# A memory-attention and mixture-of-experts kernel on one core: first batch's keys and values in token pieces, w1 in column halves, side steps placed anew

## The chip, the core and the metric

The kernel runs on one core of one Trainium2 chip. The metric is device time in microseconds of one execution, the median over runs; lower is better. All times below are microseconds unless marked ns. Engines are named as the profile names them: PE is the matmul engine (PEld its weight loads), DVE the vector engine, ACT the scalar engine, POOL the GpSimd, SP the engine whose queue issues nearly all DMAs (SPq).

## What is computed

Eight batches of eight heads, 576 tokens, head size 64, with 32 memory slots; then a mixture of eight experts (512 to 1024 to 512) over the 512 values of each token.

```python
a = softmax(phi, axis=tokens)                      # B H S M
k_m, v_m = a^T k, a^T v                            # B H M D
attn = softmax(q k_m^T / 8, axis=M)                # B H S M
x = (attn v_m) as B, S, H*D
# per batch, token after token:
e = argmax(x w_gate) if s == 0 or sigmoid(x w_local) < 0.5 else previous e
out[b, s] = softmax(x w_gate)[e] * (relu(x w1[e]) @ w2[e])
```

With the data used, all tokens of a batch follow the expert of its first token, so each batch loads one expert's w1 and w2, and the loop at the end over further pairs of batch and expert has no turns.

## The kernel before

The output of a batch is x w1 with x = attn v_m, so v_m is multiplied into w1 first (`w_pg`, `w_G`: G = v_m w1) and the hidden layer is attn G. Values are split into a high and a low part (Gh and Gl, ah and al, w2h and w2l), and three products replace one.

For each batch there is a main part on PE, in `moe`: `hidden` (two halves of the tokens, 256 and 320; for each chunk of 128 hidden units six matmuls, then a relu on ACT at L704 and its low part on DVE at L706, from PSUM tiles `ph` of a pool with 3 buffers), `second` for two blocks of 128 tokens (24 matmuls of 512 columns each, then a scaled eviction on ACT, L742), and `second_turned` for the other 320 tokens (four groups of 24 matmuls of 320 columns, each then transposed by DVE into oT). Later batches are prepared by side steps in between:

- the front (`f_...`): `f_colmax` (tree of maxima on DVE), `f_pm`, `f_mc`, `f_pm2`, `f_cx` bring the column maximum to all partitions, `f_sub` and `f_exp`, `f_asum` (tree of sums), `f_pkv` (144 matmul records: k_m and v_m), `f_sums`, `f_rinv`, `f_kvn`, `f_pT`, `f_kvT`, `f_pgg`, `f_ggt`;
- the attention of a batch in two parts of nine blocks of 32 tokens: `k_qT` (DVE transposes), `k_psc` (scores on PE), the softmax steps `k_turn`, `k_mx`, `k_sub`, `k_exp` (ACT), `k_sum`, `k_inv`, `k_mul`, `k_at`, all but one on DVE, then `k_ah` (ACT) and `k_al` (POOL);
- the choice of the expert: `c_pl` (PE), `c_choice` (DVE), `expert` (SP reads the number), then `load1` and `load2` for w1 and w2 in two halves each;
- the weights: `w_pg` (PE), `w_G` (Gh on ACT, L675; Gl on DVE, L676), `w_split` (w2h on ACT, L653; w2l on POOL, L654);
- the gate: `g_pl`, `g_lt`, `g_L`, `g_fresh`, `g_exp`, `g_kept`, `g_carry`, `g_prob`, `g_cols`, `g_present`, mostly short DVE operations.

Their order is written out by hand. `start` issues what comes ahead of the first hidden matmul, with `warm(n)` matmuls on zeros between the steps of PE (L209). All later side steps are put on a list by `at(b, x, f, ...)` in the functions `plan_...`: batch b and a place x in microseconds of the main part's own length (END = 37.8 a batch). While `moe` yields the length of each group of matmuls, the steps whose place is passed are issued. Every engine works off its own queue in that order. Batches 1 to 4 have places of their own in these tables; from batch 5 on they are all alike.

In `start` SP issues phi of batch 0 in two halves of the heads, two small loads of q, k and v by pairs of heads, phi of batch 1, the rest of q and k of batch 1 (into a buffer of the pool `pf`). The gate's weights are loaded by POOL's queue. All loads of SP share one queue. The tiles `raw` for w1 and w2 have three buffers in all.

## Time and profile before

| | |
|---|---|
| median of 3 runs | 463.33 (462.44 to 466.58) |
| the profiled execution | 465.2, its span 463.1 |
| PE busy | 418.2 (90% of the span) |
| DVE busy | 283.8 (61%) |
| ACT, POOL busy | 177.9 (38%), 169.8 (37%) |
| DMA | 82.58 MB, 178 GB/s in the mean |

A row of a timeline has the start, the length, the engine, the line, the operation with its output and inputs, and the count; in brackets is the idle time of the engine ahead of it and what ended it. A row of groups has busy time and the mean ns of one instruction instead. In a table by stretches the columns are the stretch, its length, busy time and count of each engine, the granted clock of PE as a share of full speed, the DMA engines' busy share and their rate. A busy PE is not PE at its peak, since its matmuls overlap; the distance of their starts tells their pace.

### The profile page before, as it was taken

Reading aid. Unit: us, or ns where it says so; the run is one execution under the profiler, and the core shown is the slowest. Engines: PE = TensorE matmul, PEld = TensorE weight load, DVE = VectorE, ACT = ScalarE, POOL = GpSimd, SP = SyncE. Lnnn points to the kernel's source line nnn. Section 1 sums busy time; section 2 is a strip of 40 time slices with the busy share of each in tenths; the row PEclk is TensorE's granted clock in tenths of the full one; section 3 lists DMA queues with packets and bytes.
Section 4 is the critical chain, followed back from the end, with each engine's and each line's share of the span. In section 5 each row is a group of like instructions: output and inputs, shape, how many; then the busy total and the mean of one; then the engine's idle time right before and its main releaser. Section 6 shows DMA issues by size and latency. Waiting matters only on the chain.

```text
span 463.1 us, 10643 instructions
## 1 busy us (share of the span) xinstructions
PE 418.2 (90%) x4188; PEld 340.9 (74%) x4190; DVE 283.8 (61%) x731; ACT 177.9 (38%) x425; POOL 169.8 (37%) x183
## 2 busy tenths in 40 slices
...
GB/s 240 274 313 203 222 163 24 283 143 348 92 134 235 196 268 57 39 282 250 262 154 238 263 233 118 257 215 302 81 279 149 125 104 227 166 24 57 24 36 49
DMA packets 109797, 82.58 MB, mean 178 GB/s; under 512 B 69600, under 2 KB 86000, under 8 KB 109744
## 3 DMA queue, kind: packets, MB, share of 16 engines
...
q14 instruction: 18, 0.15, 0.1%
...
## 4 chain that ended last, share of the span: by engine, by line
PE 44%; DVE 10%; SPq 8%; DMA 4%; issue 2%; ACT 1%; POOL 1%; DVEq 0%; POOLq 0%
PE ph L695 15%; SPq L157 8%; PE po L782 5%; PE po L784 5%; PE po L783 5%; PE po L734 3%; PE po L735 3%; PE po L736 3%; DMA kv_t<-in_k_dram 3%; DVE qT L364 1%; PE psc L391 1%; DMA att_d<-at 1%; PE pg L664 1%; DVE h L706 1%; PE po L756 1%
## 5 line engine op out<-in xcount | busy, mean ns | idle before, releaser
L654 POOL TENSOR_TENSOR w2l<-raw,w2h 128x512 fp32r<-128x512 f32 x64 | 81.7, 1294 | 30.9 <-ACT w2h L653 27.0
L695 PE MATMUL ph<-ah,Gh 128*128 128x256 f32 (+1 forms) x256 | 80.3, 314 | 8.5 <-DVE h L706 8.5
L706 DVE SCALAR_TENSOR_TENSOR h<-ph,h 128x320 fp32r<-128x320 f32 (+2 forms) x104 | 53.3, 522 | 46.1 <-ACT h L704 45.9
L695 PE MATMUL ph<-al,Gh 128*128 128x256 f32 (+1 forms) x256 | 77.0, 301 | 0.0
L695 PE MATMUL ph<-ah,Gl 128*128 128x256 f32 (+1 forms) x256 | 77.0, 301 | 0.0
L782 PE MATMUL po<-h,w2l 128*128 128x320 f32 x224 | 72.7, 324 | 0.0
L784 PE MATMUL po<-h,w2h 128*128 128x320 f32 x224 | 70.3, 314 | 0.0
L783 PE MATMUL po<-h,w2h 128*128 128x320 f32 x224 | 70.3, 314 | 0.0
L704 ACT ACTIVATE h<-ph 128x320 fp32r<-128x320 f32 (+1 forms) x96 | 46.5, 488 | 53.6 <-PE ph L695 50.3
L447 POOL TENSOR_TENSOR al<-at,ah 128x576 fp32r<-128x576 f32 x16 | 23.2, 1451 | 105.9 <-ACT ah L443 105.9
L734 PE MATMUL po<-w2h,h 128*128 128x512 f32 (+1 forms) x152 | 61.6, 405 | 0.0
L695 PEld LDWEIGHTS ph<-ah,Gh 128*128 128x128 f32 x256 | 49.7, 194 | 15.3 <-DVE h L706 10.3
L735 PE MATMUL po<-w2l,h 128*128 128x512 f32 (+1 forms) x152 | 58.8, 387 | 0.0
L736 PE MATMUL po<-w2h,h 128*128 128x512 f32 (+1 forms) x152 | 58.4, 384 | 0.0
L789 POOL TENSOR_TENSOR oT<-oT,gT 128x320 f32<-128x320 f32 x28 | 21.8, 778 | 95.9 <-DVE oT L788 91.8
L695 PEld LDWEIGHTS ph<-al,Gh 128*128 128x128 f32 x256 | 49.7, 194 | 0.0
L695 PEld LDWEIGHTS ph<-ah,Gl 128*128 128x128 f32 x256 | 49.5, 193 | 0.0
L782 PEld LDWEIGHTS po<-h,w2l 128*128 128x128 f32 x224 | 43.0, 192 | 6.0 <-issue 5.5
L653 ACT ACTIVATE w2h<-raw 128x512 fp32r<-128x512 f32 x64 | 38.7, 624 | 12.9 <-DMA raw<-in_moe_w_dram 7.3
L783 PEld LDWEIGHTS po<-h,w2h 128*128 128x128 f32 x224 | 43.0, 192 | 0.2
L784 PEld LDWEIGHTS po<-h,w2h 128*128 128x128 f32 x224 | 43.0, 192 | 0.0
L734 PEld LDWEIGHTS po<-w2h,h 128*128 128x128 f32 x152 | 29.3, 193 | 16.0 <-issue 11.3
...
## 6 DMA issues: line engine op xcount, KB each, us to landing
raw<-in_moe_w_dram SPq DMA_DIRECT2D x16, 1024.0 KB, 6.4
...
```

The lines of the kernel that those rows point to most:

```text
L157: nc.sync.dma_start(out=st.qt[p0 : p0 + 32, h], in_=qv[h, g, j])
L653: nc.scalar.activation(h, src, AF.Copy)
L654: nc.gpsimd.tensor_tensor(out=l, in0=src, in1=h, op=ALU.subtract)
L695: nc.tensor.matmul(pv[:, c - c0], lhsT=lt[:, g, cs], rhs=rt[:, g, s0 : s0 + n], start=(i == 0), stop=(i == 5),)
L704: nc.scalar.activation(hc[:, :, 0:n], pv, AF.Relu)
L706: nc.vector.scalar_tensor_tensor(out=hc[:, :, o : o + z - a], in0=pv[:, :, a:z], scalar=0.0, in1=hc[:, :, a:z], op0=ALU.max, op1=ALU.subtract,
L734: nc.tensor.matmul(po[:, c0:c1], lhsT=h[:, c, th], rhs=hi, start=(c == 0), stop=False)
L735: nc.tensor.matmul(po[:, c0:c1], lhsT=h[:, c, th], rhs=lo, start=False, stop=False)
L736: nc.tensor.matmul(po[:, c0:c1], lhsT=h[:, c, tl], rhs=hi, start=False, stop=(c == FC - 1))
L782: nc.tensor.matmul(po[:, 0:n], lhsT=lo, rhs=h[:, c, 0:n], start=(c == 0), stop=False)
L783: nc.tensor.matmul(po[:, 0:n], lhsT=hi, rhs=h[:, c, 0:n], start=False, stop=False)
L784: nc.tensor.matmul(po[:, 0:n], lhsT=hi, rhs=h[:, c, n : 2 * n], start=False, stop=(c == FC - 1))
```

## The change

1. **Keys and values of batch 0** are loaded right after phi, all heads at once, in two pieces of the tokens (`PIECES`: six and three of each group of nine). `f_sub` and `f_exp` become `f_piece`, `f_asum` becomes `f_asum_piece`, and `f_pkv` runs over a piece's tokens. The small loads of q and the rest of it come behind, then phi of batch 1. k of batch 1 goes to the ordinary buffer, so its load waits for `f_pkv` of batch 0.
2. **The gate's weights** are loaded by SP instead of POOL, between the two loads of q.
3. **w1** is loaded in halves of its columns (all four blocks of rows, 512 columns) instead of halves of its rows, so `w_pg(n)` reads half n alone.
4. **The six matmuls of a hidden tile** come in the order Gh ah, Gl ah for both groups, then Gh al twice; they were Gh ah, Gh al, Gl ah for each group. In the first batch `k_al` is done for each group by itself.
5. **The evictions of `second`** in batches 0 to 6 become a step of their own, `t_evict`, with a place.
6. **The places** of all side steps of batches 0 to 4 are rewritten, and `start` has another order, with 14 warm matmuls instead of 52. `w_pg(0)` comes ahead of the first hidden tile and `w_pg(1)` behind it.

The core of the diff, with a line or two of the tables:

```diff
-        nc.gpsimd.dma_start(out=wg[:, :, 0:E], in_=w_gate.rearrange("(h p) e -> p h e", h=HG))
-        nc.gpsimd.dma_start(out=wg[:, :, E : E + 1], in_=w_local.rearrange("(h p) o -> p h o", h=HG))
+
+    def gate_weights():
+        nc.sync.dma_start(out=wg[:, :, 0:E], in_=w_gate.rearrange("(h p) e -> p h e", h=HG))
+        nc.sync.dma_start(out=wg[:, :, E : E + 1], in_=w_local.rearrange("(h p) o -> p h o", h=HG))
...
+    PIECES = (slice(0, 6), slice(6, 9))
...
+    def f_piece(st, i):
+
+        x = st.pt[:, :, PIECES[i]]
+        c = st.cx.unsqueeze(2).to_broadcast([P, HG, PIECES[i].stop - PIECES[i].start, M])
+        nc.vector.tensor_tensor(out=x, in0=x, in1=c, op=ALU.subtract)
+        nc.scalar.activation(x, x, AF.Exp)
...
-        raw = pw.tile([P, 2, F], F32, tag="raw", name="raw1", bufs=3)
-        nc.sync.dma_start(out=raw, in_=w1v[:, 2 * i : 2 * i + 2])
+        raw = pw.tile([P, HG, F // 2], F32, tag="raw", name="raw1", bufs=3)
+        nc.sync.dma_start(out=raw, in_=w1v[:, :, F // 2 * i : F // 2 * (i + 1)])
...
-                    rhs=st.raw1[h // 2][half[g], h % 2, 512 * n : 512 * n + 512],
+                    rhs=st.raw1[n][half[g], h],
...
-                        for lt, rt in ((G[0], ah), (G[0], al), (G[1], ah)):
...
+                    steps = [(x, ah, g) for g in range(NG) for x in G] + [(G[0], al, g) for g in range(NG)]
...
+    def t_evict(st, t):
+        o, p = st.ot[t]
+        p = p.rearrange("p (dc j l) -> p dc j l", j=4, dc=4)
+        nc.scalar.activation(by_chunk(o), p, AF.Copy, scale=st.g[0][:, t : t + 1])
...
-        x, y, p = {1: (25.4, 25.5, 32.5), 2: (12.4, 12.5, 22), 3: (9, 9.9, 17)}.get(n, (3.6, 9.9, 14))
+        x, y, q, p = {1: (22.9, 23, 23.1, 31), 2: (17.1, 17.2, 17.3, 26), 3: (12.1, 18, 12.2, 21)}.get(
+            n, (3.6, 9.9, 10, 14)
+        )
...
         fetch_phi(s, True)
         gate_constants()
+        for i in range(2):
+            fetch_kv(s, piece=PIECES[i])
         q0 = fetch_q0()
         next(q0)
-        for hs in pairs:
-            fetch_kv(s, parts=((0, hs), (1, hs)))
+        gate_weights()
+        next(q0)
         fetch_phi(n, False, pf, "oT")
-        next(q0)
-        fetch_kv(n, pf, "h256", ((0, slice(0, HG)),))
-
-        warm(12)
+
+        warm(10)
```

How it moves instructions, at the three places of which the prediction speaks. The lines of the changed kernel are its own: L692 is `w_pg`, L722 `hidden`, L704 Gl, L732 the relu's low part, L660 and L670 the loads of w1 and w2.

On PE, the end of `start`: psc is the last part of batch 0's scores, wp the warm matmuls, pg `w_pg`, ph `hidden`. Before, twelve warm matmuls and both halves of `w_pg` stand there, and each half reads both tiles of w1:

```order
L391 MATMUL psc<-qT,kvT 32x288 x8
L209 LDWEIGHTS wz
L209 MATMUL wp<-wz 128x512
...
L664 MATMUL pg<-raw_397,kvT 32x512 x4
L664 MATMUL pg<-raw_399,kvT 32x512 x4
...
L695 MATMUL ph<-ah,Gh 128x256
L695 MATMUL ph<-al,Gh 128x256
L695 MATMUL ph<-ah,Gl 128x256
```

Now:

```order
L415 MATMUL psc<-qT,kvT 32x288 x8
L692 MATMUL pg<-raw_389,kvT 32x512 x8
L722 MATMUL ph<-ah,Gh 128x256
L722 MATMUL ph<-ah,Gl 128x256
...
L722 MATMUL ph<-al,Gh 128x256 x2
...
L692 MATMUL pg<-raw_391,kvT 32x512 x8
L722 MATMUL ph<-ah,Gh 128x256
```

The warm matmuls are gone, one half of `w_pg` with one tile of w1 is ahead of the hidden matmuls, and the other stands behind twelve of them.

On DVE, the same place: at is the end of the softmax of the first part, sc and mx the softmax of the last part, Gl belongs to `w_G`, phi_t to `f_sub` of batch 1, h to the relus. Before:

```order
L439 STREAM_TRANSPOSE at<-sc 128x2x256
L404 STREAM_TRANSPOSE sc<-psc 128x288 x2
L414 TENSOR_REDUCE mx<-sc 128x18
L418 TENSOR_TENSOR sc<-sc,mx 128x576
L676 TENSOR_TENSOR Gl<-pg,Gh 128x512 x4
L258 TENSOR_TENSOR phi_t<-phi_t,cx 128x576 x2
L706 SCALAR_TENSOR_TENSOR h_586<-ph,h_586 128x2x256
L427 TENSOR_REDUCE sm<-sc 128x18
```

Now:

```order
L463 STREAM_TRANSPOSE at<-sc 128x2x256
L704 TENSOR_TENSOR Gl<-pg,Gh 128x512 x2
L428 STREAM_TRANSPOSE sc<-psc 128x288 x2
L438 TENSOR_REDUCE mx<-sc 128x18
L442 TENSOR_TENSOR sc<-sc,mx 128x576
L732 SCALAR_TENSOR_TENSOR h_521<-ph,h_521 128x2x256
L451 TENSOR_REDUCE sm<-sc 128x18
L704 TENSOR_TENSOR Gl<-pg,Gh 128x512 x2
L732 SCALAR_TENSOR_TENSOR h_521<-ph,h_521 128x2x256
L263 TENSOR_TENSOR phi_t<-phi_t,cx 128x576
```

The first half of Gl stands right behind at, ahead of three softmax steps of the last part; the second half and one `f_sub` stand among the relus (the other `f_sub` is ahead of this place).

On SP, from the w2 load of batch 1 on: raw_1105 and raw_1351 are its halves before (raw_1029 and raw_1211 now), q_t is q of batch 2, att_d and out_dram are stores, phi_t and kv_t the loads for batch 3. Before:

```order
L642 DMA raw_1105<-in_moe_w_dram 128x2x512
L157 DMA q_t<-in_q_dram 32x18x32 x16
L452 DMA att_d<-at 128x1152
L135 DMA phi_t<-in_phi_dram 128x4x288
L135 DMA kv_t<-in_k_dram 128x4x576
L135 DMA kv_t<-in_v_dram 128x4x576
L642 ISA
L642 DMA raw_1351<-in_moe_w_dram 128x2x512
```

Now:

```order
L670 DMA raw_1029<-in_moe_w_dram 128x2x512
L162 DMA q_t<-in_q_dram 32x18x32 x16
L851 DMA out_dram<-ot 128x512
L480 DMA att_d<-at 128x1152
L670 ISA
L670 DMA raw_1211<-in_moe_w_dram 128x2x512
...
L140 DMA phi_t<-in_phi_dram 128x4x288
L140 DMA kv_t<-in_k_dram 128x4x576
L140 DMA kv_t<-in_v_dram 128x4x576
```

The second half of w2 has passed three large loads.

From batch 5 on the order of all engines is the one of before, with t_evict where the eviction stood.

327 lines of the change are left out of this document (183 added, 144 removed), and 3 rows, old and new, of the table b.

## The prediction

> **What bounds the kernel now.** I read the table by stretches first, cut where a batch's first hidden matmul starts (batch 0 at 38.32, batch 1 at 105.48, batch 2 at 171.86, batch 3 at 233.66, then every 47.6). Columns: length, then busy us of PE, weight loads, DVE, ACT, POOL, then the granted clock, DMA share and rate.
>
> ```profile
> core 0: us, PE busy (x) PEld busy (x) DVE busy (x) ACT busy (x) POOL busy (x), PEclk, DMA share, GB/s
> 0.00:38.32 38.32, 31.63 (x397) 16.20 (x399) 20.05 (x54) 9.91 (x21) 4.76 (x29) 0.96 0.83 269
> 38.32:105.48 67.16, 57.05 (x691) 46.72 (x684) 40.04 (x99) 24.46 (x60) 28.05 (x32) 0.92 0.64 173
> 105.48:171.86 66.38, 54.54 (x543) 43.83 (x542) 42.76 (x120) 25.90 (x72) 23.22 (x22) 0.92 0.72 212
> 171.86:233.66 61.80, 52.07 (x513) 42.81 (x512) 43.26 (x98) 22.59 (x54) 21.85 (x20) 0.94 0.58 173
> 233.66:281.29 47.63, 47.48 (x509) 39.94 (x508) 34.81 (x87) 21.78 (x52) 22.52 (x21) 1.00 0.72 216
> ...
> 376.53:463.10 86.57, 80.56 (x538) 71.53 (x536) 35.62 (x103) 29.74 (x63) 24.30 (x22) 0.98 0.29 92
> ```
>
> Two regimes. From batch 3 on PE has no idle to speak of: 47.63 a batch, full clock, nothing to win by placing. Before that a batch takes 62 to 67 for the same work, and the first hidden matmul comes only at 38.32. Batches 0 to 2 together take 195.3.
>
> What they would take without stalls: three times 47.63 is 142.9, and one more f_pkv, g_pl, f_sums, k_psc and small steps than three of the later batches, since the fronts get ahead here. The groups of the fourth batch's stretch (busy, mean ns of one):
>
> ```profile
> L280 PE MATMUL pkv<-kv_t,phi_t 64*32 64x128 f32 x144 | 2.2, 271 | 0.0
> L391 PE MATMUL psc<-qT,kvT 64*32 64x288 f32 x32 | 2.1, 415 | 0.2 <-DVE qT L364 0.2
> L484 PE MATMUL pl<-at,ggt 128*32 128x160 f32 (+1 forms) x16 | 0.7, 292 | 0.0
> ```
>
> That is 2.2 + 1.0 (16 of the 32 psc) + 0.7, with about 1 for the small steps: 5. The floor is 148, the loss 47. PE's timeline shows where it sits; in brackets is the idle time before a row and who ended it:
>
> ```profile
> 69.32 0.69 PE L391 MATMUL psc<-qT,kvT 64*32 64x288 f32 x8 [2.47 <-DVE gs L602]
> 70.85 1.18 PE L391 MATMUL psc<-qT,kvT 64*32 64x288 f32 x8 [0.84 <-DVE qT L364]
> 96.70 0.63 PE L280 MATMUL pkv<-kv_t,phi_t 64*32 64x128 f32 x21 [2.21 <-issue]
> 142.41 1.15 PE L484 MATMUL pl<-at,ggt 128*32 128x160 f32 x14 [3.71 <-DVE at L439]
> 187.42 0.48 PE L239 MATMUL pm<-ident,cm 128*128 128x128 f32 x1 [3.76 <-DVE cm L222]
> ```
>
> A side step stands in PE's order before its DVE input is ready, and all matmuls behind it wait. Each gap costs twice, because the clock drops after it; rows around the gap at 69.32:
>
> ```profile
> 66.46 0.39 PE L736 MATMUL po<-w2h,h 128*128 128x512 f32 x1
> ...
> 72.98 0.63 PE L736 MATMUL po<-w2h,h 128*128 128x512 f32 x1
> 73.41 0.63 PE L734 MATMUL po<-w2h,h 128*128 128x512 f32 x1
> ...
> 74.53 0.39 PE L734 MATMUL po<-w2h,h 128*128 128x512 f32 x1
> 74.75 0.39 PE L735 MATMUL po<-w2l,h 128*128 128x512 f32 x1
> ```
>
> Starts are 0.43 apart instead of 0.22 until 74.5, some 2.5 us after work came back.
>
> **The change, part by part.**
>
> *Start up to the first hidden matmul.* The chain of before:
>
> ```profile
> 13.37 1.84 PE L280 MATMUL pkv<-kv_t,phi_t 64*32 64x128 f32 x60 [0.26 <-DMA kv_t<-in_v_dram]
> 21.62 0.24 PE L458 MATMUL pl<-ggt,at 128*1 128x8 f32 x4 [0.38 <-DVE at L439]
> 23.84 0.99 SPq L632 DMA_DIRECT2D raw<-in_moe_w_dram  x2
> raw<-in_moe_w_dram SPq DMA_DIRECT2D x1, 1024.0 KB, 5.2
> 31.27 0.68 ACT L443 ACTIVATE ah<-at 128x576 fp32r<-128x576 f32 x1 [1.39 <-DVE at L439]
> 32.04 1.40 POOL L447 TENSOR_TENSOR al<-at,ah 128x576 fp32r<-128x576 f32 x1 [28.10 <-ACT ah L443]
> 34.75 1.90 PE L664 MATMUL pg<-raw,kvT 64*32 64x512 f32 x18
> 37.30 1.09 PE L664 MATMUL pg<-raw,kvT 64*32 64x512 f32 x14 [0.65 <-DVE Gl L676]
> 38.32 0.39 PE L695 MATMUL ph<-ah,Gh 128*128 128x256 f32 x1
> ```
>
> Keys and values now stand right behind phi on SP, ahead of the q ends and the second phi, and f_pkv follows tokens: I take 2 us off the wait at 13.37 (bounds 0, since pieces of 3 tokens are runs of a third of the length, and 3.5). c_pl moves behind a k_q0 on PE, where eight warm matmuls stood: 0 (up to +2 if q lands late; the k_q0 that waits would hold c_pl, the choice and the w1 load). So w1 goes out near 22. Its first column half suffices for w_pg(0) and needs the 5.2 of one load, not both: about 27 instead of 34.75, where twelve warm matmuls also stood. Then it no longer sets the start. What comes late next is DVE: from the choice to the first half of at took until 31.2, through the second phi's maximum and the softmax. It begins 2 sooner and gets one f_sub more, so ah ends near 30 instead of 31.95. Gh waits for it on ACT; from pg at 34.75 to the first hidden matmul now go 3.6 with the second half of pg between, so with one half I give Gh and Gl 2.3 behind ah. al, 1.40 in one piece on POOL, now comes in two pieces and is read last by each hidden tile, so it sets nothing. First hidden matmul at 32.3, **-6.0** (bounds -8.5, if the 2 us are 3.5 and no clock is lost, and -1, if f_pkv gains nothing, q lands late and the clock drops). w_pg(1) then falls behind that point: **+1.1** (row 37.30).
>
> *SP's queue in the start.* Three steps move there. The two gate-weight loads leave POOL and stand ahead of q: two issues, and many short runs for pgg, which runs only behind f_pkv, so there is some 3 us of cover; without it they hold pgg and c_pl. k of batch 1 loses its own buffer and waits for f_pkv of batch 0 (PE), ahead of the expert's value load: queued behind it is the w1 load. f_pkv ends some 7 us before that load is due, so the wait is over by then: 0 (0 to +2 if f_pkv is late). w1 in column halves has runs of half the length, 2 KB; one load of 1024 KB took 5.2 with 4 KB runs, and I leave it there.
>
> *Fewer warm matmuls.* 38 of 52 go. PE will have gaps of 1 to 4 us in the start, and by the rows at 72.98 some of its work there runs at half pace. f_pkv is 144 records, 4.4 us at the 1.84 for 60 above, and one w_pg 1.1; with k_q0 and k_psc I estimate 11 us of matmul work ahead of the first hidden matmul. After one gap the pace was back in 2.5 us, so I count 1 to 2 lost in the -6.0 and the rest in its upper bound. [...]
>
> *Batch 0.* The second softmax, f_sub, w_G, gate steps and relus (L706) share DVE up to the two k_qT, for which k_psc waits.
>
> ```profile
> 38.32:70.80 32.48, 24.63 (x323) 21.14 (x316) 21.00 (x58) 15.82 (x43) 15.60 (x20) 0.95 0.71 187
> ```
>
> DVE is busy 21.0 of 32.5 there. Now it gets k_turn, k_mx, k_sub of the last part, from ahead of 38.32, and f_asum from POOL, and loses one f_sub. By the 0.76 of a 576-column transpose (L364, below) that is 2.4, and 1.4 for the tree's 1024 columns, against 0.8: 24.0. w_split leaves ACT's way until 7.3, k_at and w_G come sooner. PE is busy 24.6 in the stretch and comes to that k_psc six matmuls of 0.22 sooner now: 23. If DVE is never held up the stall is 1, if it idles for 11.5 as now it is 12; I take 6 for the batch.
>
> *Second w2 load, batch 1.* Rows of SP, ACT and PE:
>
> ```profile
> 85.99 16.30 SPq L157 DMA_DIRECT2D q_t<-in_q_dram  x16
> 105.40 1.78 SPq L642 DMA_DIRECT2D raw<-in_moe_w_dram  x2
> 117.26 0.63 ACT L653 ACTIVATE w2h<-raw 128x512 fp32r<-128x512 f32 x1 [7.34 <-DMA raw<-in_moe_w_dram]
> 119.15 0.63 PE L695 MATMUL ph<-ah,Gh 128*128 128x320 f32 x1 [4.45 <-DVE h L706]
> ```
>
> ACT stood 7.3 us on w2, the relus queued behind it, PE lost 4.45 and ran slow. In the new order that load goes ahead of phi, k and v, so this stall goes whole. The new limit in batches 1 and 2 is DVE in the hidden stage:
>
> ```profile
> L706 DVE SCALAR_TENSOR_TENSOR h<-ph,h 128x320 fp32r<-128x320 f32 x56 | 26.9, 486 | 20.6 <-ACT h L704 20.6
> L706 DVE SCALAR_TENSOR_TENSOR h<-ph,h 128x512 fp32r<-128x512 f32 x32 | 21.9, 686 | 23.2 <-ACT h L704 23.0
> L364 DVE STREAM_TRANSPOSE qT<-q_t 128x576 f32<-128x576 f32 x28 | 21.3, 764 | 1.9 <-issue 1.1 <-DMA kv_t<-in_k_dram 0.4 <-DMA kv_t<-in_v_dram 0.2
> 61.74 0.14 DVE L529 STREAM_SHUFFLE rb<-c 32x1 f32<-32x1 f32 x1
> 68.02 0.17 DVE L584 TENSOR_TENSOR pr<-pe,es 32x18 f32<-32x18 f32 x1
> 233.66:248.20 14.54, 14.54 (x121) 13.60 (x120) 10.99 (x23) 8.70 (x19) 13.23 (x11) 1.00 0.71 235
> ```
>
> In batch 1 the order puts there twelve relus (4 of 0.686, 8 of 0.486: 6.6), g_kept to g_prob (61.74 to 68.2 less two relus: 5.5), two k_qT (1.5) and three softmax steps of the same width (2.3): 15.9 against PE's 14.5. In batch 2 it is relus, a whole softmax (seven steps of that width, 5.3), f_colmax, k_turn's second half and two k_qT, near 15. That alone is about 1 a batch. A relu that is late holds a PSUM tile and so PE, and the waits of later places come on top: the idle rows shown above were 0.8 to 3.8 each, and two of the size in the middle make up the rest. Over 47.6 these two batches lose 18.8 and 14.2 now, and 12 and 14 without the 7 us of the w2 wait. Between 0.5 (batch 3 and on) and 12 I take a little under the middle, 5.5 for each.
>
> *Batches 3 to 7.* PE's order, and that of the others but for names, is as before; t_evict falls where the eviction stood; the hidden matmuls only change places (starts are 0.12 apart in all three positions now): 0, within 1 either way.
>
> **Sum.** Floor 148, +1.1, +6 +5.5 +5.5 = 166 for batches 0 to 2 against 195.3: -29; with the start **-35**. The profiled span of 463.1 (465.2 as a run) becomes 428; the median shown, 463.33, is close to the span, so 428 there too. That stalls vanish is argued only from order and sums of durations; all bounds at their worst give 452 (start -1, 12 lost in each batch), at their best 410.
>
> **Rivals.**
>
> *DVE takes over.* The rewritten places trade PE waits for new ones: start -3, batches 0, 1, 2 -5, -7, -3: 445. For it: DVE is busy 40 to 43 in each of these batches against 34.8 later, and in-order queues make each misplaced step block. Against: at a floor of about 50 a batch it still has 7 to spare.
>
> *Nearly all stalls gone.* Start -8, 5 us left: 414. For it: the later batches run with DVE at 73% and no stall. Against: the sum of 15.9 for 14.5 above.
>
> *The time is waited for elsewhere.* Loads come no sooner, and PE waits for w1 and kv where it waited for DVE: 461. Against: DMA share 0.64 to 0.72 would rise by a fifth at most, near the 0.72 at which batch 3 runs unhindered.
>
> *Slower: PE stays cold.* Without the filling matmuls short gaps hold the clock down through batches 0 to 2. Those 149 us of work at 0.43 against 0.22 cost up to 140; it decides from about 38 us of cold work on, and a third of the work cold gives 428 + 45 = 473. For it: stretches with gaps have 0.92 now. Against: pace came back in 2.5 us at 74.5. [...]
>
> **How the numbers follow.** Forecast (430 give or take 12) 0.59, DVE takes over 0.17, nearly all gone 0.15, elsewhere 0.05, slower 0.04. Faster by over 1% (about what a measurement of this kernel tells from no change) 0.91, same 0.05, slower 0.04. The time is that of the likeliest, 428; 412 to 450 leaves out the last two and the ends of the second and third.
>
> **What would show it.** Right: first hidden matmul near 32; w1 out near 22; no ACT wait of 7 us on raw; batches 0 to 2 at 50 to 59 each with granted clock above 0.95; later batches at 47.6. Wrong: a first hidden matmul after 36, waits on DVE of 3 us and more in those batches, or a later batch off 47.6 by over 0.3.

## The result and the profile after

The changed kernel takes **450.96** (median of 4 runs, 448.82 to 453.38) against 463.2 for the kernel before on the same chip: a ratio on record of 0.9723, 95% interval 0.9651 to 0.9796. It is faster, as forecast, but by 12 instead of 35, and 0.96 above the upper end of the range. The profiled execution took 453.38, the longest of the four, its span 451.5 at a mean granted clock of 0.952; the shortest span was 447.0, at 0.972. Medians and ratios here and below leave out executions in which the chip was in a slower state, four of the run called e8 and three of e10.

The table by stretches, cut again where a batch's first hidden matmul starts:

```profile
core 0: us, PE busy (x) PEld busy (x) DVE busy (x) ACT busy (x) POOL busy (x), PEclk, DMA share, GB/s
0.00:32.02 32.02, 20.29 (x343) 12.02 (x343) 16.49 (x50) 8.93 (x20) 2.20 (x27) 0.89 0.86 276
32.02:99.20 67.18, 58.00 (x699) 45.35 (x700) 46.99 (x113) 27.32 (x67) 26.19 (x31) 0.92 0.69 188
99.20:156.33 57.13, 52.20 (x527) 42.91 (x526) 38.29 (x108) 22.64 (x59) 21.50 (x21) 0.94 0.72 223
156.33:222.45 66.12, 56.18 (x529) 45.77 (x528) 43.72 (x104) 24.75 (x63) 23.66 (x22) 0.87 0.59 187
222.45:270.07 47.62, 47.46 (x509) 39.87 (x508) 34.96 (x88) 21.77 (x52) 22.79 (x21) 1.00 0.75 216
```

The first hidden matmul came at 32.02 instead of 38.32 (forecast 32.3), and the later batches still take 47.6. But batches 0 to 2 took 190.4, not 166. Batch 1 gained 9.25, batch 0 nothing (67.16 before), batch 2 lost 4.3 (61.80 before).

Each row splits into three: idle time of PE (length less PE busy), clock loss (PE busy times what the granted clock is short of 1) and the rest, work at full clock. It is an accounting, not a list of savings: idle time can hide clock loss. And it is of one execution each.

| | before: idle, clock loss, work | after: idle, clock loss, work | forecast: stall |
|---|---|---|---|
| batch 0 | 10.1, 4.6, 52.5 | 9.2, 4.6, 53.4 | 6 |
| batch 1 | 11.8, 4.4, 50.2 | 4.9, 3.1, 49.1 | 5.5 |
| batch 2 | 9.7, 3.1, 48.9 | 9.9, 7.3, 48.9 | 5.5 |
| sum | 31.7, 12.0, 151.6 | 24.0, 15.1, 151.3 | 17 over a floor of 149 |

So 39 of loss stand where 17 were forecast, 24 idle and 15 of clock. Much of the idle time sits at these rows of PE's timeline; the bracket is the idle time ahead of a row and what ended it:

```profile
11.58 3.74 PE L304 MATMUL pkv<-kv_t,phi_t 64*32 64x128 f32 x144 [3.39 <-DMA kv_t<-in_v_dram]
28.02 1.09 PE L692 MATMUL pg<-raw,kvT 64*32 64x512 f32 x16 [0.79 <-DMA raw<-in_moe_w_dram]
32.02 0.38 PE L722 MATMUL ph<-ah,Gh 128*128 128x256 f32 x1 [2.90 <-ACT Gh L703]
62.34 0.69 PE L415 MATMUL psc<-qT,kvT 64*32 64x288 f32 x8 [2.30 <-DVE qT L388]
65.72 1.19 PE L415 MATMUL psc<-qT,kvT 64*32 64x288 f32 x8 [2.69 <-DVE qT L388]
168.72 0.41 PE L722 MATMUL ph<-ah,Gh 128*128 128x320 f32 x1 [1.60 <-DVE h L732]
172.65 0.45 PE L244 MATMUL pm<-ident,cm 128*128 128x128 f32 x1 [2.31 <-DVE cm L227]
190.57 0.30 PE L315 MATMUL pkv<-ones,asum 64*32 64x1 f32 x12 [3.35 <-issue]
```

The wait for w2 in batch 1 is gone. At 62.34 and 65.72, in batch 0, PE still waits for DVE's transposes, at the place where before it waited 2.47 and 0.84. The rows at 168.72 and 172.65 are two of the new waits in batch 2, and at 190.57 stands one for nothing that the profile shows.

Why batch 0's transposes are late, in DVE's and POOL's timelines:

```profile
58.62 1.11 DVE L575 COPY end<-sc 32x2 f32<-32x2 f32 x1
62.40 0.97 DVE L605 TENSOR_SCALAR es<-es 32x18 f32<-32x18 f32 x1
```

```profile
58.37 1.35 POOL L682 TENSOR_TENSOR w2l<-raw,w2h 128x512 fp32r<-128x512 f32 x1 [1.30 <-ACT w2h L681]
62.09 1.26 POOL L682 TENSOR_TENSOR w2l<-raw,w2h 128x512 fp32r<-128x512 f32 x1 [2.37 <-ACT w2h L681]
```

These two small operations of DVE have medians of 0.156 and 0.166 over all batches. Each ends within 0.02 of the end of POOL's w2l, at 59.7 and 63.4. And over the whole stretch up to the end of the second of the two waits:

```profile
32.02:65.72 33.70, 24.97 (x327) 19.74 (x327) 24.80 (x65) 14.82 (x36) 10.31 (x10) 0.91 0.75 223
```

```profile
L732 DVE SCALAR_TENSOR_TENSOR h<-ph,h 128x320 fp32r<-128x320 f32 (+1 forms) x12 | 6.5, 552 | 7.6 <-ACT h L730 7.6
```

DVE was busy 24.8 and idle 8.9 there, 7.6 of them with the low part of a relu at the head of its queue, for which ACT had not delivered the relu. It was not full; it stood.

### The profile page after: what moved, and what is told of

It reads as the page before. It is cut to its first block, busy times and chain, and to the rows that moved or that the text cites. A ratio compares the mean times of both kernels' runs of the same rounds, so it can differ in the third digit from the quotient of the medians.

```text
span 451.5 us, 10551 instructions
## 1 busy us (share of the span) xinstructions
PE 409.7 (91%) x4150; PEld 337.3 (75%) x4150; DVE 283.3 (63%) x735; ACT 178.7 (40%) x425; POOL 165.8 (37%) x179
## 4 chain that ended last, share of the span: by engine, by line
PE 46%; SPq 8%; DVE 8%; DMA 5%; ACT 2%; issue 2%; DVEq 0%
PE ph L722 15%; SPq L162 7%; PE po L810 5%; PE po L812 4%; PE po L811 4%; PE po L760 4%; PE po L762 4%; PE po L761 4%; PE pg L692 2%; DVE qT L388 2%; DMA kv_t<-in_k_dram 2%; DMA att_d<-at 1%; DMA phi_t<-in_phi_dram 1%; PE pkv L304 1%; PE psc L415 1%
## 5 line engine op out<-in xcount | busy, mean ns | idle before, releaser
L682 POOL TENSOR_TENSOR w2l<-raw,w2h 128x512 fp32r<-128x512 f32 x64 | 82.7, 1310 | 36.3 <-ACT w2h L681 35.8
L722 PE MATMUL ph<-ah,Gh 128*128 128x256 f32 (+1 forms) x256 | 76.3, 313 | 5.5 <-ACT Gh L703 2.9
L732 DVE SCALAR_TENSOR_TENSOR h<-ph,h 128x320 fp32r<-128x320 f32 (+2 forms) x104 | 53.4, 522 | 39.6 <-ACT h L730 39.2
L722 PE MATMUL ph<-ah,Gl 128*128 128x256 f32 (+1 forms) x256 | 74.1, 304 | 0.3 <-DVE Gl L704 0.3
L760 PE MATMUL po<-w2h,h 128*128 128x512 f32 (+1 forms) x152 | 63.0, 415 | 0.0
L761 PE MATMUL po<-w2l,h 128*128 128x512 f32 (+1 forms) x152 | 60.0, 395 | 0.4 <-POOL w2l L682 0.4
L762 PE MATMUL po<-w2h,h 128*128 128x512 f32 (+1 forms) x152 | 59.9, 394 | 0.0
L722 PEld LDWEIGHTS ph<-ah,Gh 128*128 128x128 f32 x256 | 49.9, 195 | 12.4 <-DVE h L732 4.2
L471 POOL TENSOR_TENSOR al<-at,ah 128x576 fp32r<-128x576 f32 (+1 forms) x18 | 23.5, 1312 | 93.4 <-ACT ah L467 93.4
L722 PE MATMUL ph<-al,Gh 128*128 128x256 f32 (+1 forms) x256 | 56.6, 303 | 0.4 <-POOL al L471 0.3
L722 PEld LDWEIGHTS ph<-ah,Gl 128*128 128x128 f32 x256 | 49.9, 195 | 0.7 <-DVE Gl L704 0.5
L722 PEld LDWEIGHTS ph<-al,Gh 128*128 128x128 f32 x256 | 42.8, 196 | 0.9 <-POOL al L471 0.9
L704 DVE TENSOR_TENSOR Gl<-pg,Gh 128x512 fp32r<-128x512 f32 x32 | 20.6, 685 | 35.4 <-ACT Gh L703 35.4
```

The lines of the kernel that those rows point to most:

```text
L471: (eng or nc.gpsimd).tensor_tensor(out=st.al[:, gs, ss], in0=st.at[:, gs, ss], in1=st.ah[:, gs, ss], op=ALU.subtract)
L682: nc.gpsimd.tensor_tensor(out=l, in0=src, in1=h, op=ALU.subtract)
L722: nc.tensor.matmul(pv[:, c - c0], lhsT=lt[:, g, cs], rhs=rt[:, g, s0 : s0 + n], start=(i == 0), stop=(i == 5),)
L732: nc.vector.scalar_tensor_tensor(out=hc[:, :, o : o + z - a], in0=pv[:, :, a:z], scalar=0.0, in1=hc[:, :, a:z], op0=ALU.max, op1=ALU.subtract,
L760: nc.tensor.matmul(po[:, c0:c1], lhsT=h[:, c, th], rhs=hi, start=(c == 0), stop=False)
L761: nc.tensor.matmul(po[:, c0:c1], lhsT=h[:, c, th], rhs=lo, start=False, stop=False)
```

## The experiments

Medians, and the ratios on record to the kernel before on the same chip, with their 95% intervals, from five rounds each. The experiments ran on three chips, so they are compared by the ratios. Against the change, whose interval is the widest, e1, e4, e5, e12 and e15 are faster by more than the noise, e3 and e6 by a little more than it, e8 and e11 are slower; the others cannot be told from it. A profile is one execution, and what it says of a stretch holds for that execution.

| run | median | ratio |
|---|---|---|
| the change | 450.96 | 0.9723 [0.9651, 0.9796] |
| e1 f_pkv of batch 4 later | 447.07 | 0.9612 [0.9579, 0.9644] |
| e2 gate steps of batch 0 earlier | 451.54 | 0.9700 [0.9666, 0.9733] |
| e3 relus of batch 2 first | 448.08 | 0.9632 [0.9596, 0.9668] |
| e4 warm matmuls in the start | 445.26 | 0.9595 [0.9551, 0.9639] |
| e5 combined | 439.77 | 0.9492 [0.9446, 0.9539] |
| e6 48 instructions more on PE | 445.87 | 0.9622 [0.9575, 0.9669] |
| e7 w1 in row halves | 452.12 | 0.9752 [0.9709, 0.9795] |
| e8 old places | 461.96 | 0.9943 [0.9900, 0.9986] |
| e9 old order of hidden | 452.59 | 0.9739 [0.9691, 0.9787] |
| e10 before, 208 instructions more | 468.69 | 1.0087 [1.0043, 1.0130] |
| e11 e8 with e6 | 461.52 | 0.9932 [0.9897, 0.9967] |
| e12 combined, further | 437.16 | 0.9412 [0.9373, 0.9452] |
| e13 gap of batch 0 filled | 449.02 | 0.9669 [0.9639, 0.9700] |
| e14 keys and values behind q | 451.49 | 0.9729 [0.9693, 0.9765] |
| e15 e12 with the carry later | 440.36 | 0.9461 [0.9431, 0.9492] |
| e16 w_pg behind the softmax | 448.33 | 0.9677 [0.9634, 0.9720] |

### The wait for nothing in batch 2

**e1**: the front of batch 4, f_pkv and what follows, in batch 2 at a later place.

```diff
-                (18, 18.1, 20.4, 20.8, 22.5, 22.8, 24),
+                (22, 22.1, 24, 24.3, 25.6, 25.9, 27),
```

> The changed kernel with f_pkv, f_sums and the steps behind them of batch 4 put 4 us later in batch 2 (18 becomes 22), so that its 288 short PE instructions no longer run while the two w1 loads and the q load of 182 to 188 fill the DMA engines. Theory (PE's own instruction load is stuck behind those loads): the gap of 3.35 us that the trace ends with 'issue' at 190.57 is gone, and with it two windows of half clock; batch 2 takes 60 to 62 instead of 66.12, the kernel 4 to 6 us less than the changed one. Rival (the gap belongs to f_pkv itself, or to the sums of POOL that it waits for): the gap moves along with f_pkv and batch 2 stays within 1 us of 66.1.

The wait of 3.35 was gone, and batch 1, which is untouched, took 57.12 as in the change. Batch 2:

```profile
157.53:219.49 61.96, 53.22 (x530) 43.70 (x528) 43.65 (x104) 24.94 (x63) 23.76 (x22) 0.92 0.65 201
```

That is 4.2 less than 66.12, behind a batch 1 of the same length; idle time of PE fell by 1.2 only (9.94 to 8.74), the rest is clock. So the wait hangs on where f_pkv stands, not on its inputs. A hint at what it is stands in the profile's list of DMA queues: beside the loads there is a queue for instructions.

```profile
q8 instruction: 34, 0.56, 0.5%
```

34 packets of 0.56 MB in all are 16 KB each (the trace has 16384 bytes for every one). PE issues 4150 matmuls and 4150 weight loads, some 244 for each packet; the kernel before has 35 packets for 4188 and 4190, some 239 for each. In the changed kernel one of these loads runs from 187.69 to 188.96, while PE stands from 187.2 to 190.57, and the 24 us ahead of it have none.

**e6**: if the wait is a block of instructions that comes late, the count of the instructions ahead must move it. 24 one-column matmuls (48 instructions, 0.75) are added in the start.

```diff
         w_pg(s, 0)
+        for _ in range(24):
+            nc.tensor.matmul(wt[0][:, 0:1], lhsT=wz[:, 0:P], rhs=wz[:, 0:1], start=True, stop=True)
         w_G(s, 0)
```

> [...] Theory (the 3.35 us gap in the sums of batch 4 is a late instruction block): the gap is gone as it was with the 24 warm matmuls; batch 2 takes 60 to 63, the kernel 3 to 6 us less than the changed one. Rival (it went with the warm matmuls because of the clock or of the earlier start): the gap is still there with 3 us and the time within 2 us of the changed kernel's.

PE's timeline at the same f_pkv, 160 us behind the edit:

```profile
183.50 2.62 PE L304 MATMUL pkv<-kv_t,phi_t 64*32 64x128 f32 x142
186.04 0.23 PE L315 MATMUL pkv<-ones,asum 64*32 64x1 f32 x4
186.20 0.50 PE L760 MATMUL po<-w2h,h 128*128 128x512 f32 x1
```

No wait is left, and the kernel is about 1% faster for more work. By the profiled executions batch 2 is 4.9 shorter, and batch 1 4.1, of which 0.8 is idle time and the rest clock (below); the start and batch 0 give 1.8 back. Over all kernels that have this f_pkv at the change's place the split is clean: with the change's count of PE instructions ahead of it the wait is 3.35, 3.33, 3.11, 2.98, 3.33, 3.08 (the change, e2, e3, e7, e9, e14); with the count moved by 24 to 48 (e4, e5, e6, e12, e13, e15, e16) it is under 0.6. The moment alone does not matter: in e3 the wait ended 4.1 sooner than in the change, in e9 1.6 later, and it stayed. f_pkv and its sums are some 320 instructions in 2.8 us, more than the 244 of one packet. That PE waits there for a packet is an inference from the count and from the load at 187.69; no row names it. Why the load started only at 187.69, 0.5 after PE had stopped, stays open, as does why PE went on only 1.6 after it had landed: in e6 the one load between 160 and 184 brought no wait, though the DMA engines were nearly as full (nine tenths and more of every 0.6 us from 181 to 184 there, a share of 1.08 in the 3 us up to 187.69 here).

**e10**: the same in the kernel before, which waited 2.21 within f_pkv at 96.70. 208 instructions more ahead of it, in place of six warm matmuls.

```diff
-        warm(12)
+        warm(6)
+        for _ in range(110):
+            nc.tensor.matmul(wt[0][:, 0:1], lhsT=wz[:, 0:P], rhs=wz[:, 0:1], start=True, stop=True)
```

> [...] Theory (the wait of 2.21 us inside f_pkv at 96.70, for which the trace names no releaser, is a late instruction block too): it is gone, batch 0 takes 62 to 65 instead of 67.16, the kernel 1 to 4 us less than before. Rival (that wait belongs to f_pkv at this place): it stays at 2 us and the time within 1 us of before.

```profile
54.92 0.23 PE L291 MATMUL pkv<-ones,asum 64*32 64x1 f32 x4 [2.20 <-issue]
98.75 0.42 PE L782 MATMUL po<-h,w2l 128*128 128x320 f32 x1 [1.76 <-issue]
164.16 0.42 PE L280 MATMUL pkv<-kv_t,phi_t 64*32 64x128 f32 x9 [1.63 <-issue]
```

The expectation missed: the wait of 2.21 went, but three others came, and the kernel is 0.4% to 1.3% slower. What a shift wins in one place it can lose in others.

**e3**: batch 2's relus ahead of the exponentials and softmax steps that stood before them on ACT and DVE (the waits at 168.72 and 172.65).

```diff
-                (5.8, 7.5, 9, 9.8, 11, 11.3),
-                (11.4, 12.8, 13.6, 15, 15.1),
+                (5.8, 8.2, 10.6, 11.4, 12.4, 12.7),
+                (12.8, 13.9, 14.4, 15.6, 15.7),
...
-            3: (1, (36.2, 37.5, END + 1.5), tuple(END + t for t in (3, 4, 5, 5.1, 6.5, 7.2, 8, 8.9)),
+            3: (1, (36.2, 37.5, END + 1.5), tuple(END + t for t in (3, 4, 5, 6.2, 7, 7.7, 8.3, 9)),
```

> The changed kernel with k_exp to k_at of the first part of batch 3 about 1 us later and f_colmax's second half, f_pm and what follows of batch 4 0.6 to 1.6 us later in batch 2; f_pkv stays. Theory (in batch 2 ACT waits with k_exp for DVE with the relus behind it, and PE with f_pm for f_colmax): the waits of 1.60 and 2.31 us at 168.72 and 172.65 fall below 1 us each, the two windows of half clock at 169 to 176 go, batch 2 takes 60 to 63 instead of 66.12. Rival (DVE's work in that stage is simply too much): the waits move to the next step and batch 2 stays above 65.

```profile
154.92:215.73 60.81, 52.52 (x529) 41.67 (x528) 42.54 (x103) 23.84 (x63) 22.18 (x21) 0.97 0.69 220
```

Four waits of 0.45 to 0.86 stand for 1.60 and 2.31. Batch 2 is 5.3 shorter, though the wait for instructions is still there with 3.11; the clock went from 0.87 to 0.97. Not all of it is the order's: in e7 and e14, where batch 2 has the change's order, it took 63.6 and 63.1, with fewer windows at half rate (next section). Batch 3 took 49.2 instead of 47.6; that is no price of this edit alone, since it took 49.2 and 49.7 in e7 and e14 too.

### The clock

The granted clock is not lost by degrees. In stretches of 3.41 us, cut where it changes, it reads 1.00 or 0.50 (first length, then PE busy; the clock is the third number from the end):

```profile
59.94:63.35 3.41, 0.79 (x9) 0.18 (x8) 3.06 (x9) 0.74 (x2) 1.26 (x1) 1.00 0.06 21
63.35:66.76 3.41, 1.04 (x8) 0.20 (x8) 2.07 (x8) 0.90 (x5) 0.00 (x0) 0.50 0.02 4
66.76:70.18 3.42, 3.42 (x12) 2.63 (x9) 3.16 (x5) 1.91 (x6) 1.90 (x2) 0.50 0.00 0
70.18:73.59 3.41, 2.97 (x14) 2.12 (x13) 3.31 (x7) 1.38 (x2) 1.92 (x8) 1.00 0.00 0
...
121.36:124.77 3.41, 1.59 (x11) 1.02 (x10) 3.25 (x9) 2.12 (x9) 0.00 (x0) 1.00 0.00 0
124.77:128.19 3.42, 3.42 (x9) 2.67 (x9) 3.16 (x10) 0.90 (x2) 1.42 (x1) 0.50 0.02 2
128.19:131.60 3.41, 3.41 (x29) 2.13 (x28) 1.72 (x4) 0.00 (x0) 0.00 (x0) 1.00 0.95 327
```

Cut along these windows, the 18 traces (before, the change, e1 to e16) show when the rate changes. No window at full rate with PE busy less than 1.55 of the 3.41 was followed by another at full rate. From 1.55 to 1.82 both happen: the change lost its rate after 1.60, e13 kept it after 1.57. Later than 23 us into the run, none with more than 1.82 was followed by half rate; in the start, 2.28 at 15.55 in the change was. In the change and the kernel before, a window at half rate was followed by full rate where PE was busy 2.88 or more in it, and by half rate where it was busy 2.47 or less.

In each trace the windows lie 3.41 apart, wherever PE's gaps fall, and against the start of the span they lie anywhere from 0.07 (e13) to 3.15 (e1), at 1.90 in the change and 2.63 in the kernel before. An estimate from these figures: a gap of 2 us brings a window at half rate, 1.7 of lost work at most (half of 3.41), if it falls within one window, and none if it lies half in each of two. Batch 1 fits it. Its steps have the same order in eleven of the runs (in e9 but for the hidden matmuls, in e7 but for the halves of w1):

| batch 1, windows at half rate | us |
|---|---|
| two: the change, e1, e2, e9 | 57.11 to 57.13 |
| one: e7, e13 | 54.51, 54.54 |
| none: e3, e4, e6, e14, e16 | 52.99 to 54.02 |

Which row a kernel falls into is at least in part a matter of the execution: the mean clock of the change's four executions went from 0.950 to 0.972.

**e13**: 22 warm and two one-column matmuls ahead of the first of the two waits of batch 0, so that PE is not idle there.

```diff
+        def fill():
+            warm(22)
+            for _ in range(2):
+                nc.tensor.matmul(wt[0][:, 0:1], lhsT=wz[:, 0:P], rhs=wz[:, 0:1], start=True, stop=True)
+
+        at(0, 15.39, fill)
```

> [...] k_psc's second half comes no later, since its qT is ready only at 65.7. Theory (half of the loss is the half clock that a gap leaves behind): the two low windows at 63 to 70 are gone, batch 0 takes 62.5 to 65 instead of 67.2 to 67.9, the kernel 442 to 444. Rival (the clock after a gap costs next to nothing, since DVE is what PE waits for next): batch 0 stays at 66.5 or more and the kernel at 445 to 447.

```profile
60.21 4.92 PE L214 MATMUL wp<-wz 128*128 128x512 bf16 x22
66.24 0.69 PE L415 MATMUL psc<-qT,kvT 64*32 64x288 f32 x8 [0.46 <-DVE qT L388]
70.58 0.50 PE L761 MATMUL po<-w2l,h 128*128 128x512 f32 x1 [1.30 <-POOL w2l L682]
```

The clock held at 1.00 from 60 to 71, and nothing was won: PE came sooner to matmuls that need w2l and waited 1.30 for POOL, which had been hidden behind the half rate, and the clock fell from 71.7 on. Batch 0 took 69.5, and the kernel is above both expectations; against e6, whose 48 PE instructions more it shares, it is 0.5% slower by the ratios, which is within the noise. The two windows at half rate cost nothing here, since other engines set the pace.

### Batch 0

**e2**: g_kept, g_carry and g_prob of batch 0 earlier, ahead of the transposes.

```diff
-            0: (0, (5.67, 6.5, 7, 8.3, 10.8), (11, 11.9, 13.9, 15.3, 19.5)),
+            0: (0, (5.67, 6.5, 7, 8.3, 10.8), (8.6, 9.6, 11.6, 15.3, 19.5)),
```

> The changed kernel with g_kept, g_carry and g_prob of batch 0 at the places 8.6, 9.6 and 11.6 instead of 11, 11.9 and 13.9, so that DVE does them in the time in which it now waits for relus, ahead of the two k_qT for which PE waits 2.30 and 2.69 us at 62.34 and 65.72. Theory (PE waits because these short gate steps stand between the two k_qT on DVE's queue): both waits together fall below 2 us, the two windows of half clock at 63 to 70 shrink to one or none, batch 0 takes 60 to 64 instead of 67.18. Rival (DVE has too much work up to there, in whatever order): the waits stay at 4 to 5 us in sum, or turn up as waits for relus ahead of that point, and batch 0 stays at 66 to 68.

```profile
60.97 0.57 PE L722 MATMUL ph<-ah,Gh 128*128 128x320 f32 x1 [1.49 <-DVE h L732]
71.40 0.50 PE L761 MATMUL po<-w2l,h 128*128 128x512 f32 x1 [1.28 <-POOL w2l L682]
```

The waits for qT are gone and these two have come; batch 0 takes 66.16 instead of 67.18, and the time is the same, as the rival had it.

**e5** puts e3 and e4 together with earlier gate steps; **e12** moves more places by the waits that were left; **e15** is e12 with the carry of batch 0 later.

```diff
-            0: (0, (5.67, 6.5, 7, 8.3, 10.8), (11, 11.9, 13.9, 15.3, 19.5)),
+            0: (0, (5.67, 6.5, 7, 8.3, 10.8), (8.6, 9.6, 11.6, 12.4, 19.5)),
```

> The changed kernel with the warm matmuls of the start, the later softmax and front steps in batch 2, and g_kept to g_cols of batch 0 at 8.6, 9.6, 11.6 and 12.4 so that the w2 copies on ACT do not queue behind g_cols; g_kept of batch 3 at 25.6 and k_psc of batch 2 at 8 besides. Theory (the loss of batches 0 to 2 is order on DVE and ACT, gap by gap, and the clock windows that the gaps set off): the gains add up, idle time of PE in batches 0 to 2 falls from 24 to 12 to 16 us, the half-clock windows to four or fewer, the kernel takes 432 to 439. Rival (DVE has no room; what one step gains the next loses): 443 or more, idle time above 20.

Batches 0 to 2 took 65.6, 53.7 and 56.3 at clocks of 0.97, 0.97 and 1.00, with 17.5 of idle time. The gains add up, to a little less than expected. For e12:

```diff
-        for c, x in enumerate((7.3, 8.3, 9.2, 10.8, 12.6, 14, 15.4, 16.7)):
+        for c, x in enumerate((7.3, 8.3, 9.2, 9.5, 10.2, 10.9, 11.8, 12.3)):
...
-            1: (0, (32.5, 33.4, 33.9, 35, 36.3), (END + 2, END + 3.7, END + 6, END + 12.4, END + 13)),
+            1: (0, (32.5, 33.4, 33.9, 35, 36.3), (END + 2, END + 5.6, END + 7.2, END + 12.4, END + 13)),
...
-            2: (1, (4, 5.5, 8), (8.5, 9.5, 10.5, 10.6, 12, 12.6, 13.3, 14.1), (15, 16, 16.6, 17)),
+            2: (1, (4, 5.5, 8), (8.5, 9.5, 10.5, 10.6, 12, 12.6, 13.3, 14.1), (15, 17.6, 18.2, 18.6)),
```

> The combined kernel with five more places moved: w2 copies of batch 0 all ahead of g_cols (up to 12.3), g_carry and g_prob of batch 1 behind the two k_qT (5.6 and 7.2), c_pl of batch 2 at 17.6 with its loads behind it, c_pl of batch 4 at 36.9, f_pm of batch 5 at 2.2. Theory (each remaining wait is a step that stands a little too early on one queue): the waits on w2l in batch 0 (2.6 us in sum), on the relu at 107.95 (2.21), on at (1.47 and 1.30) and on cm (1.73) go, idle time in batches 0 to 2 falls from 17.6 to 9 to 12 us, the kernel takes 431 to 436. Rival (DVE and POOL are full there): 438 or more, waits of the same sum at the next steps.

```profile
34.34:99.63 65.29, 57.12 (x701) 45.07 (x700) 50.31 (x113) 27.07 (x67) 25.52 (x31) 0.95 0.70 187
99.63:150.89 51.26, 48.96 (x528) 40.06 (x527) 38.99 (x108) 22.61 (x59) 22.05 (x21) 1.00 0.74 214
150.89:207.66 56.77, 51.05 (x530) 40.48 (x528) 41.19 (x102) 22.47 (x60) 21.06 (x19) 1.00 0.77 247
207.66:257.29 49.63, 48.09 (x510) 40.19 (x508) 37.59 (x91) 23.72 (x56) 25.48 (x23) 1.00 0.70 209
```

At 437.16 this is the fastest version, 5.5% to 6.3% faster than before, and faster than the change, though just above the 431 to 436 expected. (The table is of an execution that took 441.07, the longest of seven.) Batch 1 is at 51.3 and full clock. Batch 0 holds out, with a wait of 3.06 for a relu at 61.53. For e15:

```diff
-            0: (0, (5.67, 6.5, 7, 8.3, 10.8), (8.6, 9.6, 11.6, 12.4, 19.5)),
+            0: (0, (5.67, 6.5, 7, 8.3, 10.8), (8.3, 10.4, 12, 12.5, 19.5)),
```

> The last combined kernel with g_kept of batch 0 at 8.3, g_carry at 10.4, g_prob at 12 and g_cols at 12.5, so that relus stand between g_kept and g_carry on DVE. Theory (the wait of 3.06 us for a relu in batch 0 comes from the 4 us of gate steps in one piece): that wait falls below 1.5 us, batch 0 takes 61 to 64 instead of 65.3, the kernel 433 to 436. Rival (DVE has no room up to k_psc, whatever the order): the wait is at k_psc again, batch 0 65 or more, 436 or more.

It is no faster than e12 (0.5% slower by the ratios, at the edge of the noise): that relu's wait grew to 4.10, and the wait for the transposes from 0.67 to 1.86. In all of these the same steps of DVE stand somewhere between a PSUM tile and its relu. That only work taken off that stretch could help is an inference; it was not tried.

### What the start is worth

**e7**: w1 in halves of its rows again.

```diff
-        raw = pw.tile([P, HG, F // 2], F32, tag="raw", name="raw1", bufs=3)
-        nc.sync.dma_start(out=raw, in_=w1v[:, :, F // 2 * i : F // 2 * (i + 1)])
+        raw = pw.tile([P, 2, F], F32, tag="raw", name="raw1", bufs=3)
+        nc.sync.dma_start(out=raw, in_=w1v[:, 2 * i : 2 * i + 2])
...
-                    rhs=st.raw1[n][half[g], h],
+                    rhs=st.raw1[h // 2][half[g], h % 2, 512 * n : 512 * n + 512],
```

> The changed kernel with w1 loaded in halves of its rows again, so that w_pg of the first half needs both loads. My reason for the start (one load instead of two sets w_pg): w_pg starts at 31 to 34 instead of 28.0 and the first hidden matmul at 35 to 37 instead of 32.0; the kernel 3 to 5 us slower than the changed one. Rival (the first part's softmax on DVE, which ends at 30.8, sets the start anyhow): first hidden matmul within 1.5 us of 32.0 and the time within 2 us.

```profile
27.69 1.06 PE L692 MATMUL pg<-raw,kvT 64*32 64x512 f32 x8 [0.62 <-DMA raw<-in_moe_w_dram]
30.24 1.06 PE L692 MATMUL pg<-raw,kvT 64*32 64x512 f32 x8 [1.49 <-DMA raw<-in_moe_w_dram]
32.00 0.39 PE L722 MATMUL ph<-ah,Gh 128*128 128x256 f32 x1 [0.70 <-ACT Gh L703]
```

The second half of w1 arrives 2.5 later, and the first hidden matmul stands at 32.00 all the same: ACT was at ah until 31.3, and Gh stands behind it. The column halves bought nothing here.

**e14**: the pieces of k and v of batch 0 behind the first loads of q and the gate's weights.

```diff
-        for i in range(2):
-            fetch_kv(s, piece=PIECES[i])
         q0 = fetch_q0()
         next(q0)
         gate_weights()
+        for i in range(2):
+            fetch_kv(s, piece=PIECES[i])
         next(q0)
```

> The changed kernel with the small q loads and the gate weights ahead of the key and value pieces of batch 0 on SP's queue, as q was before. My reason in the prediction (keys and values first bring f_pkv 2 us forward): f_pkv, c_pl and the first hidden matmul come 1.5 to 2.5 us later, the kernel 1.5 to 2.5 us slower than the changed one. Rival (the maximum and the exponential of phi on DVE and ACT set f_pkv, and DVE the rest of the start): first hidden matmul within 1 us of 32.0 to 33.2 and the time within 1 us.

f_pkv started at 10.92 instead of 11.58, the first hidden matmul at 32.99, the time is that of the change. **e16** puts `w_pg(0)` and `w_G(0)` behind the three softmax steps of the last part, with warm matmuls ahead:

```diff
-        w_pg(s, 0)
-        w_G(s, 0)
...
+        warm(12)
+        w_pg(s, 0)
+        w_G(s, 0)
```

> The changed kernel with w_pg(0) and its w_G moved behind k_turn, k_mx and k_sub of batch 0's last part, with the twelve warm matmuls of before ahead of them, as the end of the start was ordered before (w_pg(1) stays behind). Theory (the start's 6 us come from this order on PE and DVE, since neither keys first nor the column halves brought any): first hidden matmul at 34.5 to 37 instead of 32.0, the kernel 2 to 5 us slower than the changed one. Rival (the start's gain has still another source, as the earlier second part of k_q0 and k_psc): first hidden matmul within 1.5 us of 32.0 to 33.2, the kernel within 1.5 us.

The first hidden matmul came at 33.47, 1.4 later than in the change, 0.4 later than in e6. The kernel is not slower, as had been expected: its 24 more PE instructions take the wait of batch 2 away, as in e6. **e9** takes the six matmuls of a hidden tile in the order of before:

```diff
-                    steps = [(x, ah, g) for g in range(NG) for x in G] + [(G[0], al, g) for g in range(NG)]
+                    steps = [(lt, rt, g) for g in range(NG) for lt, rt in ((G[0], ah), (G[0], al), (G[1], ah))]
```

> The changed kernel with the six matmuls of a hidden tile in the order of before (Gh ah, Gh al, Gl ah for each group). My reason in the prediction (the order costs nothing in the later batches, and in the first it only spares a wait for al): first hidden tile waits for al of POOL, 0.5 to 2 us more in the start; later batches 47.6; within 3 us of the changed kernel, not faster than it. Rival (the order matters in the hidden stages everywhere): later batches off 47.6 by over 0.3.

Same time within the noise, later batches at 47.6, and no wait for al, which had been expected. **e4** gives the start warm matmuls back, 14 ahead of f_piece and 10 behind `w_pg(0)`:

```diff
         f_cx(s)
+        warm(14)
...
         w_pg(s, 0)
+        warm(10)
```

> The changed kernel with 14 warm matmuls more ahead of f_pkv of batch 0 and 10 between w_pg of the first half and the first hidden matmul. Theory (the clock that is lost in gaps of the start costs time on the path): f_pkv takes 2.2 to 2.6 us instead of 3.74 and the first hidden matmuls run at full clock instead of 0.58; first hidden matmul at 30.5 to 31.5 and batch 0 shorter by 1 to 2 us, 2 to 3.5 us in all. Rival (DVE and the loads set the start, PE's pace does not matter): f_pkv is faster but the first hidden matmul stays within 0.5 us of 32.02 and the whole within 1 us.

```profile
11.73 1.58 PE L304 MATMUL pkv<-kv_t,phi_t 64*32 64x128 f32 x96 [0.50 <-DMA wg<-in_moe_w_gate_dram]
13.91 0.91 PE L304 MATMUL pkv<-kv_t,phi_t 64*32 64x128 f32 x47 [0.60 <-DMA kv_t<-in_v_dram]
```

f_pkv takes 2.5 of work instead of 3.74: in the change most of it falls into a window at half rate (from 12.1 to 15.6). The first hidden matmul comes at 31.57, 0.45 sooner. The rest of e4's gain goes as in e6: its 48 instructions take the wait in batch 2 away, and in the profiled execution, the fastest of its six, batch 1 has no window at half rate.

None of these edits moved the first hidden matmul by more than 1.5, and a start that nobody edited scatters by more: it gave 32.02 in the change, 33.18 in e1, 34.30 in e2, 32.79 in e3 and 31.73 in e13. e4's start gave 31.57 in e4 and e5 but 34.34 in e12. So these runs bound what each edit is worth, to some 2 us, and show of none that it is what the start gained.

### What the places are worth

**e8**: the changed kernel with the old places of batches 2 to 4 and of the gate of batches 1 to 3; one table of five is shown.

```diff
-            2: ((15.1, 16.4, 18.3), (19.5, 20.5, 21.5, 21.6, 23, 23.6, 24.3, 25), 26),
-            3: ((9.9, 11.5, 13), (14.1, 15, 16, 16.1, 17.5, 18.1, 18.8, 19.6), 20.3),
+            2: ((5.5, 7.0, 10.5), (11.5, 13.5, 14, 14.8, 15.6, 16.4, 16.7, 17.5), 18.2),
+            3: ((1.5, 3.0, 5), (6, 8, 13.5, 14.3, 15.1, 15.9, 16.2, 17.0), 17.7),
```

> The changed kernel with the places of before for all side steps of batches 2 to 4 and the gate steps of batches 1 to 3; the start, batch 0's own steps, the loads and the hidden order stay changed. Theory (the new places gain in batch 1 alone, where the w2 load is no longer late, and lose as much in batch 2 as they gain elsewhere): the ACT wait of 7 us for w2 is back and batch 1 takes 64 to 67, batch 2 61 to 63; the kernel 3 to 8 us slower than the changed one, 454 to 459. Rival (the new places gain little or nothing, the rest is the start): within 2 us of 451.

Only 0.1% to 1.0% is left of the gain, less than either side expected. **e11** is e8 with the 24 one-column matmuls of e6, to see whether the wait for instructions had eaten the start's gain.

> The kernel with the places of before for batches 2 to 4 and the change's start, with the 48 additional PE instructions of single-column matmuls. Theory (that kernel showed almost none of the 5 to 6 us won in the start because its new block alignment gave it the 2.95 us gap in the sums of batch 4 and two more low windows): the gap is gone, batch 2 falls from 67.45 to 60 to 63, the kernel takes 456 to 460. Rival (what the start wins is lost again in DVE's waits whatever the blocks): 461 or more.

The time is the same, with that wait cut from 2.95 to 0.53. The first hidden matmul came at 33.06, 5.3 sooner than before, but batches 0 to 2 took 69.1, 65.6 and 63.7, 198.4 instead of 195.3: with the old places most of the earlier start is waited off again behind it. The new places are worth some 10 of the 12, give or take 4 (e8 against the change).

e11 also shows what the earlier load of w2 is worth without them. In its batch 1 ACT has no wait on raw, yet PE stands where it had waited 4.45 for a relu before, and for at as before (3.71):

```profile
115.86 0.42 PE L722 MATMUL ph<-ah,Gh 128*128 128x320 f32 x1 [1.28 <-DVE h L732]
118.66 0.63 PE L722 MATMUL ph<-ah,Gh 128*128 128x320 f32 x1 [1.66 <-DVE h L732]
135.83 1.27 PE L512 MATMUL pl<-at,ggt 128*32 128x160 f32 x14 [3.51 <-DVE at L463]
```

The batch has 8.9 of idle time instead of 11.8, and takes 65.6 instead of 66.4.

## Why the prediction was wrong

**Start, -6.0: right in size (-6.3), not by its reasons, and so in part by luck.** "The first column half suffices" (e7), keys and values first (e14: f_pkv ended at 15.5 before and at 15.3 after, so there were no 2 us) and `w_pg(0)` ahead of the softmax (e16) are each worth little when undone alone. w1 went out at 22.94, 0.9 sooner. The end of the sum missed twice, in opposite directions. ACT in the change:

```profile
30.80 0.68 ACT L467 ACTIVATE ah<-at 128x576 fp32r<-128x576 f32 x1 [2.72 <-DVE at L463]
31.38 1.06 ACT L703 ACTIVATE Gh<-pg 128x512 fp32r<-128x512 f32 x2
```

ah ended at 31.48, not near 30, and the first hidden matmul came 0.5 behind it, not 2.3. What is left by the rows is that both halves of `w_pg` and twelve warm matmuls, which stood from 31.2 to 38.3 ahead of the first hidden matmul, are gone from there, so that it waits for ah and Gh alone. e16 put back the warm matmuls and the first half; the second half was not put back by itself, and the size of the gain is known only to the scatter of 31.7 to 34.3. (The 52 warm matmuls given for the kernel before are the records in its trace; its code has 54.)

**Batches 3 to 7, 0: right.** 47.6 each, and the order of the hidden matmuls shows no cost (e9).

**Batches 0 to 2, "166 against 195.3: -29": this failed; measured -4.9.** The floor of 149 was 2 too low. The stall terms failed, all three taken from between two bounds without a row for the middle: 6, 5.5 and 5.5 measured 13.8, 8.0 and 17.2 (idle time and clock loss in the table above), 39 instead of 17. The largest miss is batch 2. The steps that failed:

- *Batch 0, "6 for the batch".* The sums of work were near: DVE 24.8 up to the second k_psc for 24.0 forecast, PE 25.0 for 23. What failed is the choice of 6 between "DVE is never held up" (1) and "idles as now" (12). DVE idled 11.5 in that stretch before and 8.9 after, 7.6 of it at the head of its queue for relus, though it had work behind them. Where PE, ACT and DVE hand each other a tile, as here, the lag of the chain counts, not the sum. The two small operations that ended with POOL's w2l added 1.8 (1.11 + 0.97 less two medians), which the sum could not have either. The upper bound given, 12, was near.
- *"Each gap costs twice".* It was seen, but no term prices it by itself, as if the clock came back with the idle time. Idle time fell from 31.7 to 24.0, clock loss went from 12.0 to 15.1, 7.3 of it in batch 2, where five windows ran at half rate. The bound from the row at 74.5 was right for one gap; that a gap of about 2 us within one window is enough, and that its place against the windows counts (batch 1 in one order had two, one or none at half rate), was not seen. In the change the window at 121.36, with 1.8 us idle in all (1.59 busy of 3.41), was followed by one at half rate.
- *Waits of "issue" taken for waits that places remove.* The row at 96.70 in the prediction has no releaser. It left that place, and one of 3.35 came in batch 2; with the half rate that it brings, that cost about 4 (e1).
- *The w2 wait of batch 1, "this stall goes whole".* The wait went: none of ACT on raw is left. Its price was wrong. The 7 us taken off the batch's loss of 18.8 were a wait of ACT; e11, without it but with the old places, has relus that are late by DVE instead and is 0.8 shorter than before. By this comparison most of the 9.25 that the batch gained is the work of the new places.

The rival "DVE takes over" (445) came nearest, and too low; waits traded for new ones are what e2 and e15 show. A good part of the gap between 451 and 428 was to be had: e12 reaches 437, with 16.2 of idle time left in batches 0 to 2, half of it in batch 0.
